# Mamba-2 scan and hash routing on one core: the filler matmuls, the first activation table, the x loads and the last routing step moved

## The chip, the cores and the metric

The kernel runs on one core of a Trainium2 chip. A core has a TensorE (PE) for matmuls, with its weight loads shown as a row of their own (PEld), a VectorE (DVE), a ScalarE (ACT), a GpSimd (POOL) and a SyncE (SP) whose main work is to issue DMAs. Each engine runs its own instructions in order and waits on semaphores for the others. Matmuls write to PSUM, which DVE and ACT read. The metric is the device time of one execution in microseconds (us); the median of three runs of the kernel before is 257.11 us.

## The reference

Two blocks run one after the other, all in fp32. The first is a chunked state-space scan (Mamba-2) over 4 sequences x 8 heads x 768 positions, with head size 32 and state size 16:

```python
log_a = np.log(np.clip(a, 1e-06, 1.0))
for c in range(nc):                        # 24 chunks of 32
    cum = np.cumsum(la, axis=-1)
    L = np.exp(cum[..., :, None] - cum[..., None, :]) * causal
    CB = np.einsum('bhin,bhjn->bhij', Cc, Bc)
    y_intra = np.einsum('bhij,bhjd->bhid', CB * L, xc)
    y_inter = np.einsum('bhin,bhnd->bhid', Cc, state) * np.exp(cum)[..., None]
    y[:, :, sl] = y_intra + y_inter
    Bx = np.einsum('bhjn,bhjd->bhjnd', Bc, xc) * np.exp(cum[..., -1:] - cum)[..., None, None]
    state = np.exp(np.sum(la, axis=-1))[..., None, None] * state + np.sum(Bx, axis=2)
```

Its output is turned into 3072 tokens of 256 values. The second block sends each token to one of 8 experts by a hash of its id (with these constants the expert is the id modulo 8) and applies that expert's two-layer network:

```python
expert_idx = token_ids * np.int64(2654435761) % np.int64(E)
for e in range(E):
    xe = x[expert_idx == e]
    out[expert_idx == e] = np.maximum(xe @ w1[e], 0.0) @ w2[e]
```

## The kernel before

**Stages.** The scan works on half-chunks of 64 positions (`HL`) and on 24 tiles of 128 tokens, six for each sequence; the loop over tiles is `for gc in range(NCH)` (line 637). A prologue prepares the first sequence. After the loop, the experts' part runs in one fixed sequence: a small bucket of 256 tokens of one expert while the others' tokens are still gathered, then seven larger buckets, each product of which is split into seven smaller ones (class `Double`), then a last bucket of 172. Everything is under `tc.manual_schedule()`: each engine gets its instructions in the order in which the program writes them. No planner reorders them.

**Prologue.** The decay `a` is loaded (line 90), clipped on DVE (line 384), its logarithm is taken on ACT (386), and DVE sums it along the positions (`cum`, 390). A matmul with `rel_w` (395) gives the offsets, DVE adds them (397), and ACT makes two exponential factors `fac` (399, 400). `rows` (463 for the first sequence) multiplies B and C by them; `turned` (497) transposes the products on PE in halves, and ACT copies each half out of PSUM (`turn_b` line 503, `turn_c` line 510). `turn_steps` (480) turns B once more, `grams` (572) makes B·C products and `states` (536) the state updates. `steps` (433 to 442) takes the decay of whole half-chunks with four matmuls (436) and three exponentials on ACT.

Between these, `spin` (line 191) issues matmuls whose results nobody reads; they only keep PE at work. There are 6 and 4 with 128 moving columns (`ones`), then 3 and 1 with 256 columns of `cum`, which has 96 rows. An fp32 matmul shows in the profile as two matmul records.

ACT [...] loads a set for the Copy of `clear_x` (line 153), another for Ln (386) and another for Exp (399). `clear_x` writes zeros into the halves of `xall` that a head pair doesn't use.

**x.** `xall` holds three sequences' x in turn. One sequence comes in one or more DMAs of SP's queue (line 110). The first sequence's come in the prologue. The second sequence's four DMAs are asked for in tiles 0 and 1, two each. SP works in order and also stores each tile's y (line 599), a store that waits for ACT's copy of the tile.

**A tile.** Tile `gc` first issues the gram of tile `gc + 1`, whose masked product `m` DVE makes (576), then its own outputs (588, 595), which need `m` of this tile, and then one piece of preparation for the next sequence (`turn_b`, `turn_steps`, `turn_c`, `states`, `blocks`). `states` of the second sequence comes in tile 3 and is the first to read that sequence's x.

**Routing.** `routing()` (line 233) is a generator; its pieces are DVE work on the token ids. A tuple in line 664 says how many pieces go into each tile. The piece before the last gives the index lists with which tokens are gathered; the last piece (372 to 377) makes `eov`, which only a loop for left-over tokens reads.

**End.** `turn_o` (line 869) transposes finished output columns to tokens (873) into the two halves of one PSUM bank (`turns`), copies them out with ACT or DVE and scatters them to HBM by a GpSimd DMA (712). The last call handles two tiles at once.

## Time and profile before

| what | value |
|---|---|
| three runs | 257.31, 255.37, 257.11 us |
| span of the profiled execution | 260.5 us |
| PE busy | 245.8 us (94% of the span) |
| DVE, ACT, POOL busy | 167.7, 112.7, 134.7 us |
| share of PE in the chain that ended last | 71% |
| scan ends, experts' matmuls begin | at about 84.8 us |
| mean granted clock of PE | 0.985 |

The page's chain of work goes back from the last instruction to what released it, and so on to the start. A line of it holds a start in us, a length in us, and the work. Time that an engine idles outside that chain costs nothing. In the timeline, the bracket behind an instruction is the idle time of its engine just before it and who ended it. "Busy" of PE counts time with a matmul in flight, at whatever clock[...]. The profiled execution is some us longer than the three timed ones.

### The profile page before, as it was taken

Reading aid. Unit: us, or ns where it says so; the run is one execution under the profiler, and the core shown is the slowest. Engines: PE = TensorE matmul, PEld = TensorE weight load, DVE = VectorE, ACT = ScalarE, POOL = GpSimd, SP = SyncE. Lnnn points to the kernel's source line nnn. Section 1 sums busy time; section 2 is a strip of 40 time slices with the busy share of each in tenths; the row PEclk is TensorE's granted clock in tenths of the full one; section 3 lists DMA queues with packets and bytes.
Section 4 is the critical chain, followed back from the end, with each engine's and each line's share of the span. In section 5 each row is a group of like instructions: output and inputs, shape, how many; then the busy total and the mean of one; then the engine's idle time right before and its main releaser. Section 6 shows DMA issues by size and latency. Waiting matters only on the chain.

```text
span 260.5 us, 6812 instructions
## 1 busy us (share of the span) xinstructions
PE 245.8 (94%) x2629; PEld 227.3 (87%) x2629; DVE 167.7 (64%) x378; ACT 112.7 (43%) x256; POOL 134.7 (52%) x207
## 2 busy tenths in 40 slices
PE   7999879989989999999999999999999999999990
PEld 7887768878877878899999999999999999999980
DVE  5818547669664124975885797697597598684310
ACT  7354837886624123443343443443433433433120
POOL 5657172191530497519808926935864944603043
PEclk9999979999999999999999999999999999999996
DMA  6960985998785115732353254255165151001011
GB/s 113 158 113 23 164 175 125 202 217 206 234 253 188 60 40 162 262 120 99 98 193 136 64 177 182 63 181 201 40 204 200 42 184 38 20 1 41 20 42 59
DMA packets 50837, 33.21 MB, mean 127 GB/s; under 512 B 29753, under 2 KB 47186, under 8 KB 50804
## 3 DMA queue, kind: packets, MB, share of 16 engines
q1 hardware_dynamic: 47024, 24.22, 35.8%
q0 software_dynamic: 2400, 6.43, 7.8%
q10 hardware_dynamic: 1380, 2.12, 2.8%
q8 instruction: 21, 0.34, 0.6%
q14 instruction: 12, 0.10, 0.1%
HBM read 26.47 MB, written 6.42 MB: 126 GB/s over the span
## 4 chain that ended last, share of the span: by engine, by line
PE 71%; issue 11%; ACT 5%; DVE 4%; POOL 3%; DMA 2%; POOLq 1%; SPq 0%; ACTq 0%
PE o_ps L823 19%; PE sum L794 12%; PE rest L794 5%; PE gram L572 4%; PE y_ps L588 4%; PE y_ps L595 4%; PE more L794 3%; PE tp L480 3%; PE o_ps L864 3%; PE tp L497 3%; PE tp L536 2%; DMA xall<-in_x_dram 2%; POOL out_dram L712 2%; PE turns L883 2%; PE turns L873 1%
## 5 line engine op out<-in xcount | busy, mean ns | idle before, releaser
L712 POOL DMA_INDIRECT out_dram<-o_sb,idx_out x25 | 25.9, 1037 | 66.0 <-ACT o_sb L730 60.7
L823 PE MATMUL o_ps<-mixed,s 128*128 128x210 f32 (+6 forms) x168 | 37.0, 331 | 0.0
L603 POOL DMA_INDIRECT xg<-y_tokens,idx_in x25 | 26.4, 1057 | 20.0 <-ACT hd L724 13.4
L520 POOL TENSOR_TENSOR cp<-ct,step 128x256 f32<-128x256 f32 x24 | 13.9, 615 | 29.1 <-ACT ct L510 29.1
L823 PEld LDWEIGHTS o_ps<-mixed,s 128*128 128x128 f32 x168 | 27.9, 190 | 0.0
L730 ACT ACTIVATE u<-sum 128x420 f32<-128x420 f32 (+6 forms) x28 | 14.0, 500 | 23.6 <-PE sum L794 23.6
L794 PE MATMUL sum<-xmix,s 128*128 128x210 f32 (+6 forms) x112 | 23.5, 332 | 0.1
L735 DVE TENSOR_TENSOR hT<-u,rest 128x420 f32<-128x420 f32 (+6 forms) x28 | 15.8, 563 | 9.0 <-PE rest L794 8.8
L735 DVE TENSOR_TENSOR mixed<-hT,mixed 128x420 f32<-128x420 f32 (+6 forms) x28 | 20.7, 738 | 0.5
L576 DVE TENSOR_TENSOR m<-gram,causal 128x512 f32<-128x512 f32 x24 | 16.4, 686 | 5.5 <-PE gram L572 5.5
L807 DVE SCALAR_TENSOR_TENSOR mixed<-hT 128x420 f32<-128x420 f32 (+6 forms) x28 | 19.0, 719 | 1.0
L794 PEld LDWEIGHTS sum<-xmix,s 128*128 128x128 f32 x112 | 18.3, 189 | 0.9 <-issue 0.8
L598 ACT ACTIVATE y_sb<-y_ps 128x256 f32<-128x256 f32 x24 | 9.3, 387 | 22.5 <-PE y_ps L595 19.6
L730 ACT ACTIVATE o_sb<-turns 128x256 f32<-128x256 f32 x24 | 9.2, 383 | 21.8 <-PE turns L873 20.5
L595 PE MATMUL y_ps<-xall,m 128*64 128x64 f32 x384 | 16.8, 224 | 0.9 <-DVE m L576 0.8
L572 PE MATMUL gram<-ce,bt 32*64 32x128 f32 x384 | 16.9, 293 | 0.0
L595 PEld LDWEIGHTS y_ps<-xall,m 128*64 128x64 f32 x384 | 15.4, 138 | 1.4 <-DVE m L576 1.1
L730 ACT ACTIVATE xT<-turns 128x256 f32<-128x256 f32 x23 | 8.8, 383 | 17.3 <-PE turns L883 17.3
L588 PE MATMUL y_ps<-up,cp 128*64 128x128 f32 x176 | 16.2, 292 | 0.0
L730 ACT ACTIVATE p<-sum 128x420 f32<-128x420 f32 (+6 forms) x14 | 7.0, 500 | 20.5 <-PE sum L794 20.5
L735 DVE TENSOR_TENSOR hT<-p,more 128x420 f32<-128x420 f32 (+6 forms) x14 | 7.9, 564 | 12.4 <-PE more L794 12.4
L467 POOL TENSOR_TENSOR rows<-bc,fac 96x256 f32<-96x256 f32 x24 | 14.8, 648 | 1.3 <-DMA bc<-in_B_dram 1.3
(217 smaller groups left out, 594.9 us busy)
## 6 DMA issues: line engine op xcount, KB each, us to landing
w1odd<-in_moe_w_dram SPq DMA_DIRECT2D x8, 512.0 KB, 4.0
w2odd<-in_moe_w_dram SPq DMA_DIRECT2D x8, 512.0 KB, 4.4
y_tokens<-y_sb SPq DMA_DIRECT2D x24, 128.0 KB, 3.6
w1even<-in_moe_w_dram SPq DMA_DIRECT2D x6, 512.0 KB, 4.1
w2even<-in_moe_w_dram SPq DMA_DIRECT2D x6, 512.0 KB, 4.6
xall<-in_x_dram SPq DMA_DIRECT2D x12, 192.0 KB, 4.4
bc<-in_B_dram SPq DMA_DIRECT2D x4, 384.0 KB, 5.3
bc<-in_C_dram SPq DMA_DIRECT2D x4, 384.0 KB, 5.8
```

The source lines that it names most:

```text
L467: eng.tensor_tensor(out=t.rearrange("p r (h n) -> p h r n", h=H)[:, h:h + 2], in0=bcs[b][:, i, h:h + 2], in1=fac[:, i, hs].unsqueeze(3).to ...
L572: nc.tensor.matmul(out=gram[q * HL:(q + 1) * HL, g, u * P:(u + 1) * P], lhsT=bts[b][rr, 2 * c + u], rhs=ces[b][rr, :, 2 * c + u], start=Tr ...
L576: nc.vector.tensor_tensor(out=m.rearrange("p g u e i -> p g (u e i)"), in0=gram[:, :, 0:2 * P], in1=causal.rearrange("p (g x) i -> p g (x ...
L588: nc.tensor.matmul(out=y_ps[u * HL:(u + 1) * HL, :, q], lhsT=cps[b][:, q, k], rhs=ups[b][:, k].rearrange("p g (e d) -> p (g e) d", e=2), s ...
L595: nc.tensor.matmul(out=y_ps[u * HL:(u + 1) * HL, h], lhsT=m[:, g, u, e], rhs=xs[b][:, h, k], start=(k == 0 and h == 0), stop=(h == G - 1), ...
L603: nc.gpsimd.indirect_dma_start(out=dst, out_offset=None, in_=y_dram[0:n, :], in_offset=bass.IndirectOffsetOnAxis(ap=idx, axis=0), bounds_c ...
L712: st = nc.gpsimd.indirect_dma_start(out=out[:], out_offset=bass.IndirectOffsetOnAxis(ap=idx, axis=0), in_=src, in_offset=None, bounds_chec ...
L730: nc.scalar.activation(o, i, AF.Copy)
L735: eng.tensor_tensor(out=o, in0=i, in1=j, op=op)
L794: nc.tensor.matmul(out=self.banks[name][:, e * n:(e + 1) * n], lhsT=wt, rhs=mv, start=start and e == 0, stop=True, skip_group_check=True)
L807: nc.vector.scalar_tensor_tensor(out=t[:, o], in0=h[:, i], scalar=0.0, in1=h[:, k], op0=OP.max, op1=OP.subtract)
L823: nc.tensor.matmul(out=oP[v][o][:, e * n:(e + 1) * n], lhsT=wt, rhs=mv[:, c * n:(c + 1) * n], start=(j == 0 and c == 0 and i in (1, 3, 6, ...
```

## The change

Six edits, none of which alters what is computed:

- **Fillers.** `spin` uses 256 moving columns of `ones` with the full 128 rows of the identity throughout. 6 and 4 matmuls of 128 columns become 3 and 2 of 256; 3 of 256 columns of `cum` become 2; the last single one goes. They no longer read `cum`.
- **Ln's table first.** An Ln of one column into a scrap tile is put ahead of ACT's first `clear_x`, so that the first table load is Ln's. In the built program the Copy that follows needs no other set, so one of three loads is gone.
- **`steps` earlier in the data's order.** It moves from before the first transposes to between the two halves of the first one, where the single filler was.
- **x.** The second sequence's four loads are all issued in tile 0.
- **Last routing step.** It moves from tile 17 to tile 19.
- **End.** In the last `turn_o`, the second tile's transposes go to another PSUM bank ("sum") rather than to the other half of `turns`.

```diff
     clear_x(0, 0, False)
+    scrap = const.tile([P, 1], F32)
+    nc.scalar.activation(scrap, ones[:, 0:1], AF.Ln)
     clear_x(0, 1, True)
...
-    def spin(moving, n=1):
+    def spin(n, width=2):
         t = ps_y.tile([P, 512], F32, name="y_ps")
         for _ in range(n):
-            nc.tensor.matmul(out=t[:, 0:moving.shape[-1]], lhsT=ident[0:moving.shape[0]], rhs=moving,
-                             start=True, stop=True)
-    spin(ones, 6)
+            nc.tensor.matmul(out=t[:, 0:width * P].rearrange("p (w i) -> p w i", w=width), lhsT=ident,
+                             rhs=ones.unsqueeze(1).to_broadcast([P, width, P]), start=True, stop=True)
+    spin(3)
...
-    spin(ones, 4)
+    spin(2)
...
-    spin(flat(cum), 3)
+    spin(2)
...
             if (b, i, r0) == (0, 0, RS // 2):
-                spin(flat(cum))
+                steps()
...
     rows(0, 0, nc.vector)
-    steps()
     turn_b(0)
...
-        for _ in range((1, 2, 1, 0, 1, 0, 2, 2, 2, 0, 1, 0, 2, 2, 2, 1, 1, 1)[gc] if gc < 18 else 0):
+        for _ in range((1, 2, 1, 0, 1, 0, 2, 2, 2, 0, 1, 0, 2, 2, 2, 1, 1, 0, 0, 1)[gc] if gc < 20 else 0):
...
-        for i in (2 * gc, 2 * gc + 1) if gc < 2 else ():
+        for i in range(4) if gc == 0 else ():
             load_x(1, i)
...
-        tps = [turns[:, next(side)] for _ in ks]
+        tps = [turns[:, next(side)] if i == 0 else bank("sum")[:, 0:DM] for i, _ in enumerate(ks)]
```

## The prediction

> **What bounds the kernel now.** I read the page first: PE is busy 94% of a span of 260.5 us and has 71% of the chain. So PE sets the pace, and an edit pays where PE waits, where PE does useless work, or where PE runs at half clock. I then read the chain in order of time (start, length, what) over the places the change touches.

> ```profile
> 1.48 1.28 ACT L153
> 2.77 1.48 ACT xall L153
> 4.25 0.02 issue
> 4.27 1.28 ACT L386
> 5.55 0.01 issue
> 5.56 0.43 ACT a_t L386
> ...
> 7.71 2.59 PE y_ps L195 x6
> 10.30 1.51 PE tp L436 x8
> 11.81 0.73 PE tp L497 x4
> 12.54 0.91 PE y_ps L195 x2
> 13.45 2.12 PE tp L497 x12
> 15.57 1.48 PE tp L480 x24
> ...
> 27.55 0.60 SPq L110
> 28.15 0.04 issue
> 28.19 6.14 DMA xall<-in_x_dram
> ```

> To be seen: up to 6 us the chain is ACT alone, with two table loads of 1.28 us. From 7.71 on PE sets it, and 2.59 + 0.91 us of that are fillers (L195). Then the chain leaves PE for the fourth load of the second sequence's x.

> The timeline gives the rows around that wait, the wait in tile 19 and the end; the third row is the table of stretches (start:end, length, busy time by engine, then PE's granted clock, 0.50).

> ```profile
> 34.37 1.46 PE L536 MATMUL tp<-xall,bs 64*32 64x64 f32 x42 [1.33 <-DMA xall<-in_x_dram]
> ```
> ```profile
> 34.44:37.85 3.41, 3.41 (x70) 2.91 (x72) 1.74 (x7) 0.00 (x0) 2.11 (x4) 0.50 1.08 206
> ```
> ```profile
> 75.06 0.36 DVE L372 TENSOR_TENSOR past<-iota_k,tend 128x198 f32<-128x198 f32 x1
> ...
> 76.88 0.69 PE L595 MATMUL y_ps<-xall,m 128*64 128x64 f32 x16 [0.82 <-DVE m L576]
> ```
> ```profile
> 254.42 0.38 ACT L730 ACTIVATE o_sb<-turns 128x256 f32<-128x256 f32 x1 [1.36 <-DVE o_sb L732]
> 254.67 0.98 POOL L712 DMA_INDIRECT out_dram<-o_sb,idx_out  x1 [1.03 <-DVE o_sb L732]
> 255.95 0.98 POOL L712 DMA_INDIRECT out_dram<-o_sb,idx_out  x1 [0.30 <-issue]
> ```

> PE stood almost idle from 31.7 to 34.37 us and then ran at half clock for 3.41 us. In tile 19 PE waits 0.82 us for `m`, in front of which DVE did the last routing step. At the end POOL's two scatters follow each other and ACT's late copy is in time for the second.

> [...] the trace has 1.28 us three times, and I take that. [...] the clock's changes at 34.44 and 37.85 us are 3.41 apart, and the first one, at 20.79, is five windows before 37.85. [...] PE is busy 100% of 7.13 to 10.55 us, fillers mostly, and PE stays at half clock to 20.79. [...] ACT's 254.42 waits for DVE's 253.97 to end.

> **The change part by part.**

> *Ln's table.* One load goes. Afterwards ACT does: load to 2.76, scrap Ln (one column; not in the trace; the nearest, 48 columns, takes 0.21), `clear_x` to about 4.46. DVE's clip of `a_t` (4.42 to 4.84) waits for its DMA and now binds: Ln starts at 4.87 and not 5.56. Gain 0.69. The scan then ends near 6.01 in place of 6.70. The Exp load still follows Ln (5.3 to 6.6) and hides before Exp's input at about 7.1.

> *First fillers.* 6 x 128 columns become 3 x 256 (2.93 to about 2.59 us by the 256-column row), then 2 x 256, 0.86 a matmul: 1.73. PE is through near 5.95, before the new end of the scan (6.01), so they don't hold `rel` up. From there to 7.71 all moves by 0.70: the counts end at 7.0.

> *Later fillers.* 2.59 becomes 4 records of 0.432 = 1.73: gain 0.86. The last one, 0.91, goes: gain 0.91. Their removal reaches the path only if nothing else is late. `rows` on DVE takes 3.10/4 = 0.775 each, from 7.58: first half ready at 8.36, PE wants it at 8.73. Good. Then PE: transposes 0.73 to 9.46, `steps` 1.51 to 10.97, three halves of 0.71 to 13.1. The two PSUM buffers: ACT's copy of the first half ends near 10.0, `steps`' exponentials (0.62) at 11.64, the second half's copy at 12.2; each is free before PE asks. `rows` for C are ready at 9.9 and 10.7. So L480 starts at 13.1 and not 15.57: 2.47 = 0.70 + 0.86 + 0.91. Next come `states` at 15.6 (18.10 less 2.47), whose x landed at 14.31 by its semaphore; then B of the second sequence, landed at 16.59, before POOL wants it at 17.2. Nothing absolute catches it. **2.4 us**, between 1.8 (a buffer or ACT late by half a us) and 2.5.

> *Clock in the prologue.* The fillers' purpose is an earlier full clock. Both fillers of 96 rows x 256 columns left a fully busy window cold; whether 128 rows do better no row shows. Lower bound 0. Upper: if PE is at full clock from some 8 us, the second fillers, `steps`, L480, `grams`, `states` and L480 save about 0.8 + 0.7 + 0.64 + 0.46 + 0.64 + 0.58 = 3.8, of which x's landing at 14.31 and POOL's `rows` (B landed 16.59, then 2.3 us) leave some 2. I take 0.

> *x.* In before the loads start at 24.00, 25.32, 27.55 and 28.19, with y's store at 27.01 ahead of the third. Now all follow each other; with 0.9 us each, the fourth starts near 27.1 instead of 28.19. But the DMA engines are full: the packets of x run from 26.0 to 32.7 almost without a break, at a DMA share near 1. What goes is y's 128 KB in their midst (about 0.5 us) and a gap of about 0.3. So the fourth lands 0.8 earlier relative to the tile, not 1.1. **0.8 us**, between 0.3 (contention) and 1.3. y's store moves back by 0.6; its tokens are gathered only after 71 us. Behind it SP's next loads are wanted at 31.37 or later. The half clock at 34.44 cost L536, `grams`, L588 about 0.66 + 0.46 + 0.46 = 1.6 against their warm rows; with an idle stretch of 1.9 rather than 2.7 us it may not come. I count that under the range, because the timed runs are 3 us shorter than the span of this profile and may not pay it already.

> *Last routing step.* 4 DVE instructions, 75.06 to 76.24, leave the path. `m` is ready at 75.85; PE gets to L595 at 75.99 (L588 at 75.40 + 0.59). 76.88 - 75.99 = **0.9 us**. In tile 19 the step runs after `m` of tile 20 and takes 1.1 us; DVE has 0.81 to 0.96 idle in each of these tiles and the next `m` is wanted a whole tile (1.65 us) later: hidden.

> *End.* DVE's copy no longer waits for the fourth transpose in its bank: about 0.1. ACT's copy runs beside it, but POOL needs 0.98 + 0.30 for the first scatter anyway. **0.1 us**.

> Sum: 2.4 + 0.8 + 0.9 + 0.1 = 4.2. After 84.8 us PE's matmuls follow each other and the weights are asked for by the kernel's own progress, so the shift stays. 257.11 - 4.2 = 252.9.

> **Rivals.** (1) The 128-row fillers do raise the clock early: [...] against it, the busy window that stayed cold. 4.2 + 2 = 6.2: 250.9. With the half clock after x gone as well, 1.6 more: 249.3. (2) A wait takes the place: ACT, with the three exponentials now between the copies, or POOL's `rows` holds the first tiles, and x's landing hardly moves since DMA is full. Then prologue 1.0, x 0, routing 0.9, end 0: about 255.2, within 1%. Against it stand the free times above. (3) The clock turns against it: windows fall otherwise, the colder prologue lasts a window longer or one more idle window brings 3.41 us at half clock, 1.7 us each, and four bunched loads at the 1.46 DMA share of 31 us delay x by 2 us while the prologue's gain is half lost at the same wait. 257.11 - 1.2 - 0.9 + 3.4 + 1.0 = 259.4. For it: the fillers shrink by a third after `cum`; against it: PE is cold there anyway, so there is little clock to lose.

> **How the numbers follow.** Main case 0.58; (1) 0.18; (2) 0.17; (3) 0.07. The range takes in the main case's ends: least 1.8 + 0.3 + 0.8 = 2.9, most 2.5 + 1.3 + 0.9 + 0.1 + 1.6 = 6.4, with most of (1) and the lower part of (2): 249.8 to 255.6. Faster by over 1% (below 254.54): main nearly whole and (1): 0.77. Within 1%: (2) and a little of the main case: 0.17. Slower: 0.06.

> **What would show it.** Two table loads before Exp's input, Ln at 4.9; L480 at about 13.1; the clock's first record about 2.5 us earlier or, for (1), before 10 us; four x issues in a row and L536's wait ending some 3.3 us before 34.37; no DVE L372 ahead of tile 19's L595; ACT's last copy beside DVE's. Wrong it would be if L480's start moves but `states` or tile 3 doesn't, or if the scan's end stays near 84.8.

## The result, and the profile after

The changed kernel takes 253.43 us (median of 6 executions, 252.43 to 253.97), the kernel before 257.15 us beside it (6 executions, 255.37 to 261.95). The ratio is 0.987, with a 95% interval of 0.984 to 0.991: 3.7 us less, where 4.2 were forecast. Here and below the intervals leave out executions more than 1.5% above the fastest of the same kernel; the ranges in brackets take in all.

The chain of work of the changed kernel, at the places for which the prediction showed that of before (start, length, what):

```profile
0.80 3.76 DMA a_t<-in_a_dram
...
4.59 0.42 DVE a_t L386
...
7.60 1.06 DVE rows L465
...
8.70 0.55 PE tp L499 x4
...
11.81 1.55 PE tp L482 x24
...
14.42 1.15 PE tp L538 x48
```

Both table loads are gone from the head of the chain, and so are the fillers: where PE y_ps stood for 2.59 and 0.91 us, DVE's `rows` now stands ahead of the transposes. L482 (480 before) starts at 11.81, even earlier than the 13.1 that was forecast, since `steps` (0.99 us in the timeline, 1.72 before) and the first four transpose records (0.55 us, 0.88 before) ran at the full clock.

The table of stretches gives the reason (start:end, length, then busy us and instructions of PE, PEld, DVE, ACT and POOL, then PE's granted clock, DMA share, GB/s; the clock reads 1.00 ahead of its first record, which here is at 4.79, though PE ran at about half that pace there: six records of the fillers take 2.93 us before it, four take 1.04 us after it):

```profile
1.38:4.79 3.41, 3.37 (x8) 2.29 (x9) 2.32 (x6) 2.96 (x3) 2.90 (x17) 1.00 0.74 99
...
8.20:11.62 3.42, 2.69 (x24) 2.30 (x24) 3.35 (x8) 1.84 (x6) 2.40 (x27) 1.00 1.22 146
11.62:15.03 3.41, 3.35 (x70) 2.77 (x72) 1.94 (x5) 2.77 (x6) 2.67 (x5) 0.50 1.32 170
...
18.44:21.86 3.42, 2.12 (x57) 1.57 (x46) 1.90 (x8) 1.73 (x6) 2.79 (x5) 1.00 0.29 69
```

In the clock's record of both profiles, each stretch between two changes is a whole multiple of 3.41 us: 13.65, 3.41 and 218.45 us before, 6.83, 3.41, 6.83, 3.41 and 225.28 us here. "Window" stands below for 3.41 us counted from such a change. Ahead of the first record the windows are counted back from it; that they lie so there is assumed.

After a window with 3.21 us of fillers the clock came up at 4.79 us, against 20.79 in the profile of before. It fell again at 11.62 and at 21.86, each time for one window, after windows in which PE was busy for 2.69 and 2.12 us. The half clock that before had from 34.44 to 37.85 us is not there.

The timeline has the other places:

```profile
29.54 0.88 PE L538 MATMUL tp<-xall,bs 64*32 64x64 f32 x48
...
68.91 0.63 PE L597 MATMUL y_ps<-xall,m 128*64 128x64 f32 x16
69.26 0.36 DVE L374 TENSOR_TENSOR past<-iota_k,tend 128x198 f32<-128x198 f32 x1
...
245.64 0.42 DVE L733 COPY o_sb<-turns 128x256 f32<-128x256 f32 x1 [0.48 <-PE turns L874]
245.74 0.38 ACT L731 ACTIVATE o_sb<-sum 128x256 f32<-128x256 f32 x1 [0.90 <-PE sum L874]
246.34 0.98 POOL L713 DMA_INDIRECT out_dram<-o_sb,idx_out  x1 [0.92 <-DVE o_sb L733]
247.63 0.98 POOL L713 DMA_INDIRECT out_dram<-o_sb,idx_out  x1 [0.30 <-issue]
```

`states` of the second sequence (L538, first row) runs its 48 matmuls in one piece, with no wait for x. L597 in tile 19 has no bracket: its wait for `m` is gone, and the routing step runs behind `m`. At the end both copies run side by side, but POOL's two scatters still follow each other as before.

By the milestones the gain looks like this: the experts' matmuls begin at 76.8 us instead of 84.8, and take 175.3 us to the end instead of 175.7. The span fell by 8.3 us, though, and the times only by 3.7. So the profile of before isn't the typical execution, and the two pages can't be subtracted from each other. The experiments begin with that.

### The profile page after: what moved, and what is told of

Its sections match the earlier page's. It is cut to its first block, busy times and chain, and to the rows that moved or that the text cites. A ratio compares the mean times of both kernels' runs of the same rounds, so it can differ in the third digit from the quotient of the medians.

```text
span 252.2 us, 6781 instructions
## 1 busy us (share of the span) xinstructions
PE 239.0 (95%) x2615; PEld 220.6 (87%) x2615; DVE 167.8 (67%) x378; ACT 111.8 (44%) x256; POOL 135.7 (54%) x207
## 3 DMA queue, kind: packets, MB, share of 16 engines
q10 hardware_dynamic: 1380, 2.12, 2.6%
## 4 chain that ended last, share of the span: by engine, by line
PE 73%; issue 11%; DVE 5%; ACT 4%; POOL 3%; DMA 1%; POOLq 1%; ACTq 0%
PE o_ps L824 20%; PE sum L795 12%; PE rest L795 6%; PE gram L574 5%; PE y_ps L590 5%; PE y_ps L597 4%; PE more L795 3%; PE tp L482 3%; PE o_ps L865 3%; POOL out_dram L713 2%; PE tp L499 2%; PE tp L538 2%; PE turns L884 2%; PE turns L874 2%; DMA a_t<-in_a_dram 1%
## 5 line engine op out<-in xcount | busy, mean ns | idle before, releaser
L795 PE MATMUL sum<-xmix,s 128*128 128x210 f32 (+6 forms) x112 | 23.5, 332 | 0.0
L578 DVE TENSOR_TENSOR m<-gram,causal 128x512 f32<-128x512 f32 x24 | 16.4, 685 | 5.9 <-PE gram L574 5.9
L808 DVE SCALAR_TENSOR_TENSOR mixed<-hT 128x420 f32<-128x420 f32 (+6 forms) x28 | 18.2, 691 | 1.0
L600 ACT ACTIVATE y_sb<-y_ps 128x256 f32<-128x256 f32 x24 | 9.3, 388 | 17.9 <-PE y_ps L597 14.4
L597 PE MATMUL y_ps<-xall,m 128*64 128x64 f32 x384 | 16.8, 227 | 0.1
L736 DVE TENSOR_TENSOR hT<-p,more 128x420 f32<-128x420 f32 (+6 forms) x14 | 7.9, 564 | 13.2 <-PE more L795 13.2
L731 ACT ACTIVATE xT<-turns 128x256 f32<-128x256 f32 x23 | 8.8, 384 | 17.2 <-PE turns L884 17.2
L597 PEld LDWEIGHTS y_ps<-xall,m 128*64 128x64 f32 x384 | 15.5, 141 | 0.6 <-ACT xall L153 0.6
L469 POOL TENSOR_TENSOR rows<-bc,fac 96x256 f32<-96x256 f32 x24 | 15.5, 675 | 0.8 <-DMA bc<-in_B_dram 0.7
```

The lines of the kernel that those rows point to most:

```text
L469: eng.tensor_tensor(out=t.rearrange("p r (h n) -> p h r n", h=H)[:, h:h + 2], in0=bcs[b][:, i, h:h + 2], in1=fac[:, i, hs].unsqueeze(3).to ...
L578: nc.vector.tensor_tensor(out=m.rearrange("p g u e i -> p g (u e i)"), in0=gram[:, :, 0:2 * P], in1=causal.rearrange("p (g x) i -> p g (x ...
L597: nc.tensor.matmul(out=y_ps[u * HL:(u + 1) * HL, h], lhsT=m[:, g, u, e], rhs=xs[b][:, h, k], start=(k == 0 and h == 0), stop=(h == G - 1), ...
L731: nc.scalar.activation(o, i, AF.Copy)
L736: eng.tensor_tensor(out=o, in0=i, in1=j, op=op)
L795: nc.tensor.matmul(out=self.banks[name][:, e * n:(e + 1) * n], lhsT=wt, rhs=mv, start=start and e == 0, stop=True, skip_group_check=True)
```

## The experiments

The milestones of all runs' profiles, in us, for reference. "Full" is the first record of PE's full clock; L482 is the first sequence's `turn_steps` (480 in before); y0, y2 and y5 are the starts of ACT's copy of that tile's output; "rest" is from the start of the experts' matmuls to the end of the span.

| run | full | L482 | y0 | y2 | y5 | experts | rest | median of its times |
|---|---|---|---|---|---|---|---|---|
| before, first profile | 20.79 | 15.5 | 23.2 | 29.1 | 41.0 | 84.8 | 175.7 | 257.15 |
| before_again | 6.05 | 12.0 | 18.8 | 25.6 | 35.1 | 79.1 | 175.7 | (one: 256.61) |
| only_fillers | 4.6 | 12.5 | 19.7 | 27.2 | 38.5 | 82.3 | 175.7 | 256.68 |
| only_x | 5.7 | 12.0 | 18.8 | 25.3 | 33.5 | 77.8 | 175.5 | 255.07 |
| only_routing_later | 5.6 | 12.0 | 18.8 | 25.6 | 35.0 | 78.0 | 175.5 | 257.07 |
| changed, first profile | 4.79 | 11.8 | 19.0 | 27.2 | 34.6 | 76.8 | 175.3 | 253.43 |
| all_again | 6.7 | 11.6 | 18.8 | 25.6 | 33.0 | 75.8 | 175.5 | 252.84 |
| all_but_fillers | 6.3 | 11.3 | 19.2 | 26.0 | 34.1 | 76.6 | 176.4 | 254.45 |
| x_in_prologue | 6.5 | 11.7 | 19.0 | 26.7 | 34.1 | 76.3 | 175.3 | 255.66 |
| more_fillers | 4.8 | 11.6 | 18.9 | 25.5 | 33.6 | 76.2 | 175.5 | 254.42 |
| no_fillers | 16.4 | 13.2 | 20.9 | 26.6 | 35.6 | 77.8 | 175.5 | 256.62 |
| fillers_of_96_rows | 17.9 | 13.2 | 21.0 | 26.7 | 35.9 | 79.2 | 175.0 | 255.11 |
| fillers_of_128_columns | 4.25 | 11.6 | 18.8 | 27.1 | 34.5 | 77.2 | 176.2 | 254.79 |
| turn_before_states | 5.0 | 11.6 | 19.7 | 25.2 | 35.0 | 77.6 | 175.4 | 253.45 |

### One profile more of the kernel before

No edit.

> The kernel before, profiled once more, since its first profile (260.5 us of span) is 3 us longer than its timed runs. Sum theory (each edit gives what its own wait or work was worth, and the clock's window stays a bystander): L480 starts near 15.6 us, the wait for x in front of the second sequence's states is 2 to 2.7 us. Clock theory (most of the gain is full clock in the first 25 us, given by the fillers of 128 rows and 256 columns): the same start, and the first record of full clock not before 17 us, wherever the window falls; the span may be shorter by 3 us because of it.

Span 254.8 us, time 256.61. The experts begin at 79.1 us, 5.7 earlier than in the first profile of the same kernel. The difference is there at the first tile: its output is copied at 23.21 us in the first profile and at 18.76 in this one.

```profile
23.21 0.36 ACT L598 ACTIVATE y_sb<-y_ps 128x256 f32<-128x256 f32 x1
```
```profile
18.76 0.36 ACT L598 ACTIVATE y_sb<-y_ps 128x256 f32<-128x256 f32 x1
```

The stretches of both show why. First the first profile of before, where the clock came up at 20.79, then this one, where it came up at 6.05:

```profile
0.31:3.72 3.41, 2.29 (x10) 2.30 (x11) 2.33 (x6) 2.23 (x2) 2.75 (x18) 1.00 0.51 35
3.72:7.13 3.41, 3.15 (x14) 2.61 (x14) 1.82 (x6) 3.36 (x4) 1.42 (x7) 1.00 1.01 219
7.13:10.55 3.42, 3.42 (x13) 2.85 (x13) 2.79 (x5) 0.87 (x3) 3.17 (x25) 1.00 1.08 162
```
```profile
2.64:6.05 3.41, 3.41 (x17) 3.13 (x16) 1.75 (x10) 3.35 (x5) 1.93 (x10) 1.00 0.94 166
```

The fillers of 128 rows lie between 1.4 and 6.6 us in both. In the second, a window lies wholly among them; in the first, two windows share them, and the third is filled mostly by the fillers of 96 rows and doesn't raise the clock. In these two profiles of one kernel the clock came early or late (6.05 and 20.79 us) as the windows fell: the one held 3.25 us of 128-row fillers in one window, the other 2.29 and 2.71 us in two.

How much of a window must be filled can be narrowed down. In the eleven profiles with an early clock (up by 6.7 us), the window ahead of the first record holds 2.83 to 3.25 us of fillers with 128 rows; in the first profile of before the two windows hold those 2.29 and 2.71 us, and the clock stayed at half. If some 2.8 us are needed (an estimate from these figures), the old fillers come too short where the edge of the windows (the start of one, modulo 3.41 us) lies between about 0.2 and 0.8 us, as 0.31 in the first profile does, and the new ones, which go on with 128 rows after `cum`, nowhere.

The executions without a profile can be put to this test, since each one's span and mean clock are on record. The mean leaves out the time before the first record, and each fall but the last, at the end of the span, lasted one window of 3.41 us in all profiles. So the last window ends at the span less the time at half clock, which is 2 x (1 - mean) x span, and modulo 3.41 us that is the edge. For before_again it is 254.8 - 3.06, so 2.6, where the trace has 2.64; over the 14 profiles it comes within 0.3 us. Of 141 executions of before, the 33 with an edge from 0 to 0.85 us took 260.6 us in the median, the 72 with one from 1.4 to 3.0 us 256.4; the others lie between. The times follow the place of the windows, as the estimate has it. Most of the longest also have a mean clock of 0.988 or less, so a window at half clock later on, as at 34.44 in the first profile: not all of their length is the prologue's.

With an early clock, the chain of work of this profile goes straight to x's landing:

```profile
4.67 9.64 DMA xall<-in_x_dram
...
14.36 0.89 PE tp L536 x44
...
24.53 5.51 DMA xall<-in_x_dram
...
30.09 0.85 PE tp L536 x42
```

PE is at the first `states` before 14.3 us and waits for the first sequence's x. An edit to the table loads or to the fillers' length can gain next to nothing at the first tile in such an execution. And the second sequence's x is later, counted from the first tile, than in the first profile: its fourth load is asked for at 24.53, 5.4 us after y0's store (19.14), where it was 4.6 us (28.19 and 23.59).

### Single parts put into the kernel before

Fillers and the place of `steps` alone (the two hunks of the change on `spin`, its three calls, and `steps()`):

```diff
-    spin(flat(cum), 3)
+    spin(2)
...
             if (b, i, r0) == (0, 0, RS // 2):
-                spin(flat(cum))
+                steps()
```

> The kernel before with the fillers of 256 columns of ones in the smaller number, and steps between the halves; nothing else. Sum theory: the fillers' 0.86 + 0.91 = 1.8 us, so 255.3; first record of full clock at 15 us or later. Clock theory: full clock from some 5 to 8 us in most executions, 2 to 4 us in all, so 253 to 255.

256.68 us (255.36 to 259.74), ratio 0.9976 (0.9947 to 1.0005). The clock was full at 4.6 us and fell back for three windows, at 11.4, 21.7 and 31.9 us. The last fall followed a wait for x:

```profile
32.07 1.49 PE L536 MATMUL tp<-xall,bs 64*32 64x64 f32 x42 [2.20 <-DMA xall<-in_x_dram]
```

The wait for x is still there, 2.20 us, and then half clock, in which the 42 matmuls take 1.49 us, not 0.85. Alone the new fillers gain nothing in the median that can be told from zero. Where the old ones come too short, it looks different: the seven executions with a window's edge from 0 to 0.85 us took 256.6 to 258.7 us, 257.3 in the median, where before has 260.6. Whether that is an earlier clock, or the shorter prologue of a late one, these times don't tell. The mean of all executions is 256.9 us, before's in the same comparison 258.2.

x alone:

```diff
-        for i in (2 * gc, 2 * gc + 1) if gc < 2 else ():
+        for i in range(4) if gc == 0 else ():
```

> The kernel before with the second sequence's four loads of x in tile 0; nothing else. Sum theory: 0.8 us (0.3 to 1.3), so 256.3; the fourth load lands about 0.8 us earlier after tile 0's store than in the kernel before. Clock theory: 0 to 0.8 us, since the DMA engines are full; more only where the half clock after the wait does not come.

255.07 us (253.95 to 259.16), ratio 0.9928 (0.9893 to 0.9962): 1.85 us. Chain of work:

```profile
19.54 0.61 SPq L110
...
23.14 5.23 DMA xall<-in_x_dram
```

The fourth load is issued at 23.14 instead of 24.53 and lands at 28.37 instead of 30.04, 1.67 us sooner, with the first tile's output at 18.8 us in both. y5 and the experts' start follow by 1.7 and 1.3.

The last routing step alone:

```diff
-(1, 2, 1, 0, 1, 0, 2, 2, 2, 0, 1, 0, 2, 2, 2, 1, 1, 1)[gc] if gc < 18 else 0
+(1, 2, 1, 0, 1, 0, 2, 2, 2, 0, 1, 0, 2, 2, 2, 1, 1, 0, 0, 1)[gc] if gc < 20 else 0
```

> The kernel before with the last routing step in tile 19 in place of 17; nothing else. Both theories: the wait of 0.8 us in front of tile 19's L595 goes and nothing comes for it, 0.9 us, so 256.2.

257.07 us (255.09 to 262.58), ratio 0.9978 (0.9949 to 1.0007); before in the same comparison 257.83 (255.16 to 262.78). The times can't tell it from nothing, the timelines can, since both profiles agree to 0.1 us up to there. First before_again, then this run:

```profile
71.18 0.69 PE L595 MATMUL y_ps<-xall,m 128*64 128x64 f32 x16 [0.86 <-DVE m L576]
```
```profile
70.13 0.64 PE L595 MATMUL y_ps<-xall,m 128*64 128x64 f32 x16
```

L595 has no wait for `m` any more and starts 1.05 us earlier (it has no bracket); the routing step (L372) starts at 70.53 instead of 69.35, behind it. The experts begin 1.1 sooner.

### The changed kernel again, with and without its fillers

> The changed kernel as it is, beside the next three on one chip. Seen so far, each alone: x 0.9928 of before, fillers 0.9976, routing 0.9978. If the parts add (sum theory) with Ln's 0.7 us and the end's 0.1: 0.9928 x 0.9976 x 0.9978 less 0.8 us, so 0.985 of before. If they get in each other's way (x's landing for the first sequence binds the prologue whatever is done to Ln and the fillers): 0.988 or above.

252.84 us (252.14 to 253.61), ratio 0.9834 (0.9802 to 0.9866), span 251.4. Here the clock came up at 6.7 us and didn't fall afterwards. Against before_again, which also has an early clock, all up to y2 is the same: y0 at 18.8, y2 at 25.6. The 3.3 us by which the experts begin sooner come from x (2.1 by y5) and the routing step (1.1). In such a pair the prologue gave nothing. PE comes to the first `states` earlier (13.47 against 13.95), and then waits longer for x: 44 of these matmuls start at 14.49, where before_again has 14.36.

```profile
14.49 0.86 PE L538 MATMUL tp<-xall,bs 64*32 64x64 f32 x44 [0.72 <-DMA xall<-in_x_dram]
```

The changed kernel with the old fillers and the old place of `steps`:

```diff
-    spin(3)
+    spin(ones, 6)
...
-    spin(2)
+    spin(ones, 4)
...
-    spin(2)
+    spin(flat(cum), 3)
...
-                steps()
+                spin(flat(cum))
```

> The changed kernel with the fillers and steps of before. Sum theory: the 1.8 us of fillers come back, so 255.2 if the changed kernel has 253.4. Theory that the landing of the first sequence's x (14.2 us) ends the prologue once the clock is up early: the fastest executions are as fast as the changed kernel's to 0.3 us, and the medians differ by 0.6 to 1.2 us, through executions in which the clock comes up late.

254.45 us (253.96 to 256.13), ratio 0.9905 (0.987 to 0.994), 1.6 us above all_again in the same comparison. Its one profile has an early clock (6.3) and the experts beginning at 76.6, 0.8 later; its rest is 0.8 longer than all_again's. The chain of work shows where: PE waits 0.67 us for a gather of tokens that took 7.75 us to land, a wait that all_again doesn't have.

```profile
93.19 7.75 DMA xg<-y_tokens,idx_in
...
101.08 0.41 PE turns L885 x2
```

So half of the 1.6 us between these two spans comes after the scan.

No filler at all in the changed kernel:

```diff
-        for _ in range(n):
+        for _ in range(0):
```

> The changed kernel without any filler matmul; steps stays between the halves. If the fillers are mere ballast on PE's path: as the changed kernel or up to 0.5 us faster, 252.3 to 252.8. If they are what brings the full clock early: the clock comes up only with the real matmuls at 15 to 21 us, the first y is ready some 3 us later than 18.8, and the time is 255 to 257.

256.62 us (254.71 to 259.07), ratio 1.0003 (0.9976 to 1.003): the whole gain is lost. A PE row of its timeline:

```profile
8.55 0.90 PE L499 MATMUL tp<-ident,rows 96*128 96x96 f32 x4 [1.52 <-DVE rows L465]
```

The first transposes start as early as with fillers (8.55; 8.5 in all_again), but the clock came up at 16.4, L482 came 1.5 later and y0 2.1 later. The new fillers cost PE no time that anything waits for in these profiles; what they buy is the clock.

### What raises the clock: rows or columns

The new fillers have twice the columns and all 128 rows. First only the rows taken back, all fillers at 96 rows and 256 columns:

```diff
-            nc.tensor.matmul(..., lhsT=ident, rhs=ones.unsqueeze(1).to_broadcast([P, width, P]), ...)
+            nc.tensor.matmul(..., lhsT=ident[0:96], rhs=ones[0:96].unsqueeze(1).to_broadcast([96, width, P]), ...)
```

> The changed kernel with fillers of 256 columns on 96 rows in place of 128. If the number of rows decides whether a window of fillers counts as busy (96 rows stood for most of the window from 7.1 to 10.6 us that stayed at half clock in the first profile of the kernel before): the clock comes up at 15 us or later, 255 to 257. If rows don't matter: 252.8, first record at 5 to 8 us.

255.11 us (254.25 to 257.76), ratio 0.9948 (0.992 to 0.9976). The stretches:

```profile
0.87:4.28 3.41, 2.86 (x7) 1.85 (x7) 2.34 (x6) 2.78 (x3) 2.90 (x17) 1.00 0.58 53
4.28:7.69 3.41, 3.41 (x12) 2.78 (x12) 2.33 (x8) 2.29 (x5) 2.18 (x7) 1.00 1.14 244
7.69:11.11 3.42, 3.42 (x16) 3.00 (x16) 3.31 (x7) 0.81 (x3) 2.66 (x28) 1.00 1.15 158
```

PE was busy in 2.86 us of the first window and all of the next two, and the clock stayed at half up to 17.9 us. By its profile this run is like no_fillers (y0 at 21.0 and 20.9), by its times it is 1.5 us better in the same comparison; whether its other executions had an earlier clock isn't known.

Then only the columns taken back, at 128 rows (twice as many matmuls, so that the time is the same):

```diff
-    def spin(n, width=2):
+    def spin(n, width=1):
...
-    spin(3)
+    spin(6)
...
-    spin(2)
+    spin(4)
```

> The changed kernel with twice as many fillers of 128 columns, so the same moving columns in all. If the width decides [...]: some executions come up late and the median is 254 or more. If the narrow ones do as well, as in three of four profiles of kernels with the old fillers: 252.8, within 0.4.

254.79 us (253.21 to 255.39), ratio 0.9923 (0.9899 to 0.9948). By chance its windows fell almost where those of fillers_of_96_rows fell:

```profile
0.84:4.25 3.41, 2.83 (x12) 2.64 (x12) 2.35 (x6) 2.76 (x3) 2.90 (x16) 1.00 0.58 49
```

### Trying to hold the clock, and two other orders

A third filler after the exponentials, and one between the halves of the second sequence's first transposes, to keep the clock from falling at 11.6 and 21.9:

```diff
-    spin(2)
+    spin(3)
...
                 steps()
+            elif (b, i, r0) == (1, 0, RS // 2):
+                spin(1)
```

> The changed kernel with one filler of 256 columns more after the exponentials (PE waits for DVE there from 7.7 to 8.7 us) and one between the halves of the second sequence's first transposes (PE waits 0.58 us for ACT there). If the returns to half clock at 11.6 and 21.9 us cost the changed kernel time: 0.5 to 1.5 us faster. If DMA landings bind in those stretches, or the fillers delay more than they save: 0 to 0.5 us slower.

254.42 us (253.42 to 256.08), ratio 0.9908 (0.9874 to 0.9942), 1.6 above all_again beside it. The fall at 11.6 came nevertheless (the third filler ends at 7.97, and the window that counts begins at 8.2), that at 21.9 didn't; y2 was at 25.5, 1.7 before that of the changed kernel's first profile, and x's wait in tile 3 was back with 0.41 us.

Its profile (span 251.7) doesn't explain the longer times, and later falls of the clock don't either (254.25 and 254.65 us at a mean of 0.994); the cause stays open.

The second sequence's x asked for in the prologue, right after its B and C:

```diff
     load_bc(1)
+    for i in range(4):
+        load_x(1, i)
...
-        for i in range(4) if gc == 0 else ():
-            load_x(1, i)
```

> The changed kernel with the second sequence's four loads asked for in the prologue, behind the second B and C, where SP has nothing else to do from 11.7 to 19.4 us. If part of the wait for x is left in the changed kernel: up to 0.5 us faster. If it is all gone: no difference (within 0.2 us), and the four loads land near 22 us.

255.66 us (253.04 to 258.06), ratio 0.993 (0.9904 to 0.9955). The last of x landed at 25.0 us, far ahead of use, and the experts begin at 76.3, no sooner than in all_again, where x isn't waited for either. Something else got worse. Ahead of 12 of the `states` matmuls of the second group PE idles for no semaphore ("issue"). First all_again's timeline, then this run's:

```profile
19.41 0.41 PE L538 MATMUL tp<-xall,bs 64*32 64x64 f32 x12 [0.83 <-issue]
```
```profile
20.54 0.41 PE L540 MATMUL tp<-xall,bs 64*32 64x64 f32 x12 [1.77 <-issue]
```

0.94 us more; what held PE up isn't shown. But this profile is no typical execution. Its mean clock is 0.995, and only three of the 22 have 0.993 or more; these took 253.0 to 253.7 us, like the changed kernel. The other 19 have 0.970 to 0.990 and took 253.9 to 258.1 us. At these means they ran one to four windows at half clock after the first record, beyond the stretch at the end of the span, which is 1.7 to 4.8 us in the profiles. The 2 to 3 us in the times go with these falls; why they are so many isn't shown.

`turn_steps` of the first sequence's second part ahead of the first `states`, since PE waits for x there:

```diff
+    turn_steps(0, 1)
     states(0, 0)
...
-    turn_steps(0, 1)
```

> The changed kernel with the second half of turn_steps of the first sequence ahead of its first states on PE. In the last profile of the changed kernel PE waited 0.72 us at 14.5 for the first sequence's x. If that landing is the bound of the prologue: the turn fills the wait, and the first y and the end come 0.5 to 0.7 us earlier, 252.2. If something else is (ACT or DVE behind it): no difference.

253.45 us (252.78 to 254.76), ratio 0.9884 (0.9833 to 0.9934): no gain over the changed kernel (253.43 and 252.84). Against all_again the first `states` starts at 15.4 instead of 13.5, y0 at 19.7 instead of 18.8; y2 is 0.4 sooner, y5 2.0 later. In this profile the clock was at half from 11.8 to 15.2 us, so it doesn't test the order alone. No version ran faster than the changed kernel.

## Why the prediction was right, and where its reasons were not

The size was right (3.7 of 4.2), and the mechanism of two of its four terms. The largest term, the prologue, was right in what moved and wrong in why it counts. That the sum came so near is in part luck: between before_again and all_again, both with an early clock, the experts begin 3.3 us sooner by x and the routing step alone.

- **Prologue, 2.4 us: the step that failed is "Nothing absolute catches it", together with the "I take 0" for the clock.** Everything was worked from one profile, and that had a late clock. Where the clock is late after the change too, the sum comes out: in fillers_of_96_rows L482 starts at 13.24 (forecast 13.1), `states` at 15.78 (15.6), and y0 comes 2.3 us before that of the first profile. In the profiles with an early clock, x's landing at some 14.3 us catches the whole gain: y0 is at 18.8 us in before_again, only_x, only_routing_later and all_again alike, with old fillers or new, with three table loads or two. What counts in place of the sum is whether the clock comes early. With it late in before, y0 came 4.4 us later (23.2 against 18.8); late in the changed kernel without fillers, 2.1 (20.9). That fillers bring it early is shown: without any, or with 96 rows, it came at 16.4 and 17.9. That the new ones do so more often than the old rests on less: all seven profiles with new fillers of 128 rows have it by 6.7 us, of the old ones four in five, and the estimate from the windows has no place where the new ones come too short. It fits the spread of the times, too: before ran from 255.2 to 262.8 over all comparisons, the changed kernel from 252.1 to 254.0 in 12 executions. But all_but_fillers, with the old fillers, has two executions with a window's edge at 0.2 and 0.6 us that took only 254.1 and 254.5, so in the changed kernel the new fillers' share isn't settled.
- **Rival 1 (the 128-row fillers do raise the clock)** was what took place: the 128-row fillers brought the full clock at 4.79 us, and in 128 columns at 4.25, where with those of 96 rows it came at 17.9. Its time, 250.9, was too low, since it added the clock to a gain that x's landing takes away.
- **"Ln's table", 0.69.** One load of 1.28 us is gone, and the next row of ACT's timeline has Ln wait for DVE's clip:

```profile
5.04 0.42 ACT L388 ACTIVATE a_t<-a_t 96x256 f32<-96x256 f32 x1 [0.58 <-DVE a_t L386]
```

  5.04 where 4.87 was forecast, 5.56 before: 0.52, since `a` landed at 4.56. In all_again it is 4.86. The matmul of `rel` follows, 6.32 instead of 6.85. It was not tried alone; with an early clock it is hidden by x like the rest.
- **"Later fillers", 0.86 + 0.91.** Removed as forecast; the first transposes start at 8.7 where the forecast was 8.73. What the main case left out is that a clock that is up can fall again: here after windows with PE busy for 2.69 and 2.12 us. Busy time as a whole doesn't sort the windows: turn_before_states fell after one with 3.06 us, 2.14 of them transposes (L499), x_in_prologue did not after one with 1.88 us and no transpose (16.79 to 20.20). The window from 8.20 to 11.62 has 2.01 us of transposes in its 2.69, the one from 18.44 to 21.86 has 1.10 in its 2.12. With transposes left out, the windows ahead of the falls in the scan hold 0.68 and 1.02 us here and 1.07 us in the first profile of before (31.03 to 34.44); every other window at full clock in these two scans holds 2.38 us or more. Whether the transposes as such are the reason was not shown; they were not tried alone. The place of the windows goes with the falls here as well: the five profiles with the clock up by 5.0 us all have a fall behind it, the six with it up between 5.6 and 6.7 us none. The first fall costs little, because x's landing binds there (y0 19.0 against 18.8 in all_again, which had no fall); the second put y2 back, 27.2 against 25.6. That is the price of 1.7 us that rival 3 gave one window, and 1.0 of it is left where the experts begin. So rival 3 was right in part, in one of two profiles of the changed kernel.
- **x: 0.8 forecast, 1.3 to 1.85 measured.** Right in kind, mis-sized in "What goes is y's 128 KB in their midst (about 0.5 us) and a gap of about 0.3". In before_again y1's store, for which the third load stands behind, starts 4.36 us after y0's (23.50 and 19.14), not 3.4 as in the first profile, and the second load landed at 24.20, when the third had been issued only at 23.89: the DMA share is 0.11 and 0.23 in the two half microseconds from 23.5 us, and 1.27 and 0.94 in only_x. The fourth then lands 1.67 us later than in only_x. The half clock after that wait, which the forecast left under the range, is absent in before_again as well, so it is no part of this gain.
- **Last routing step: 0.9 forecast, 1.05 measured in the timeline.** Right, though the times alone don't show it; the step is also hidden where it is now, as forecast.
- **End: 0.1 forecast.** ACT's copy starts 0.10 us after DVE's rather than behind it, POOL's second scatter 1.29 after its first as before (1.28). "Rest" differs by 0.2 to 0.4 (175.7 to 175.3 and 175.5); between runs without the edit it differs by 0.2. Nothing of it can be told from zero, and it was not tried alone.
- **Rival 2, a new wait in the prologue,** is half of the truth for executions with an early clock: x's landing does hold the first tiles, but because the clock is early, not because ACT or POOL are late.

"After 84.8 us ... the shift stays" held in both profiles of the changed kernel, but not always: in all_but_fillers and fillers_of_128_columns PE waits 0.67 and 0.41 us for a gather of tokens after that.

Open: why more_fillers takes longer than its profile, why the clock falls so often in x_in_prologue, and how the 1.6 us between all_again and all_but_fillers divide over all executions. The window's edge and the falls can be worked out for each execution; whether its clock came early can only be seen in a profile, and a profile shows one.

## What to carry to other kernels

Before costing edits in a cold prologue, take a second profile of the same kernel: one that has the clock up early may be bound by something else, and the costs of the first then don't add. Fillers are bought for the clock, not for their length: here those of 128 rows brought it (4.79 us) and those of 96 did not (17.9), and by the estimate of some 2.8 us above they had to go on long enough that a window is filled wherever the windows lie. A window of mostly transposes did not hold the clock (2.01 of 2.69 us, from 8.20 to 11.62 in the changed kernel). Before explaining times by a profile, compare the mean clocks of the executions: the profile may be one of the few without a fall. A store that waits for compute, put between loads in one queue, held back the loads behind it here (the fourth landed 1.67 us later), and the DMA engines stood almost idle until that compute was done (a share of 0.11 and 0.23 in before_again).

## What the hardware showed that I had not expected

- Fillers on 96 of the 128 rows, with the kernel's other matmuls, kept PE busy for 2.86 us of one window and for two full ones without bringing the full clock; 2.83 us on 128 rows in one window did, 2.71 us didn't. Nor is it a matter of rows for every matmul: the window from 11.62 to 15.03 in the changed kernel held 3.35 us, all but 0.13 of it on 64 and 32 rows, and full clock followed.
- PE fell to half clock after windows that were anything but idle: 2.69 us and 2.12 us busy of 3.41, in turn_before_states 3.06. In all_again, windows with 2.69 and 2.46 us (13.50 to 16.91, 16.91 to 20.33) had no fall behind them. Busy time alone doesn't sort them; with transposes left out, the windows ahead of a fall in the scans of the two first profiles held 0.68, 1.02 and 1.07 us and the others at full clock 2.38 or more.
- In the pair of profiles of before, the late clock makes the first tile 4.4 us later, 1.7% of the time: more than the whole change. And where the windows fall can be worked out from an execution's span and mean clock, without a profile: within 0.3 us over the 14 profiles.
